# Two transformer layers with sliding-window attention on one core: chunks of 512 tokens, attention of a chunk between the matmuls of its left neighbour's MLP

## The chip, the cores and the metric

The kernel runs on one core of a Trainium2 chip. The metric is the device time of one execution in microseconds (us). A core has five engines with a queue of their own each, worked off in order: PE (matmul), ACT (activation functions), DVE (vector), POOL (GpSimd) and SP (here it only issues DMAs). Engines wait for each other through semaphores. Matmuls write into PSUM, eight banks of 512 fp32 columns; the other operands lie in SBUF.

## The reference

```python
def _A_ref(x, wqkv, wo):
    B, S, D = x.shape                       # 1, 2048, 576
    H = 32; Dh = D // H; W = 256
    qkv = (x @ wqkv).reshape(B, S, 3, H, Dh).transpose(2, 0, 3, 1, 4)
    q, k, v = qkv[0], qkv[1], qkv[2]
    scores = jnp.einsum("bhqd,bhkd->bhqk", q, k) * (Dh ** -0.5)
    mask = (idx[:, None] - idx[None, :] >= 0) & (idx[:, None] - idx[None, :] < W)
    p = _softmax(jnp.where(mask[None, None], scores, -1e9), axis=-1)
    o = jnp.einsum("bhqk,bhkd->bhqd", p, v)
    return o.transpose(0, 2, 1, 3).reshape(B, S, D) @ wo
def _B_ref(x, w1, b1, w2, b2):
    y = _layernorm(x, axis=-1)
    h = _gelu(jnp.einsum("bsd,df->bsf", y, w1) + b1)      # F = 4608, tanh form
    return jnp.einsum("bsf,fd->bsd", h, w2) + b2

for _ in range(2):
    x = x + _A_ref(_layernorm(x, axis=-1), A_wqkv, A_wo)
    x = x + _B_ref(_layernorm(x, axis=-1), B_w1, B_b1, B_w2, B_b2)
```

Inputs and weights are bf16. 32 heads of 18 channels; a query sees itself and the 255 keys before it. Both layers use the same weights.

## The kernel before

The tokens are 16 tiles of 128. The residual stream x_res stays in SBUF in fp32. Every operation is recorded by a small scheduler (class Sched): it notes which names a step reads and writes, derives the semaphore waits, and each engine then runs its steps in the order in which the code recorded them. So the order of recording is the order of execution on each engine.

There are four stages, one after the other: attention, MLP, attention, MLP, each over all tiles; at a seam the first tiles of the next stage are prepared in the last ones of the stage before (hooks A_HOOK_T and M_HOOK_TC).

Attention works by tile t, group g of four heads, and pair pr of two heads: 512 steps in all. A step scores (L538) multiplies the pair's keys of up to three key tiles with the queries, each head in its own 32 rows of the PE array; expo (L553, ACT) exponentiates 128 keys x up to 768 values; masks (L559 and L563, POOL) clear the triangles; pv (L580) multiplies with V, where a column of ones gives the sum of the softmax; norm (L601, L606, DVE) divides. Two score slots of two banks alternate. Between the steps come the projections of tiles to come: Q and K by tile pairs (L478, emptied by DVE at L488), V (L503, L512), the output projection (L628, L634). The layer norm is statistics (L391, L393), a square root on ACT (L410, L413), and normalisation (L421); five DMA transposes of 128x128 per tile on SP's queue (L431 for the normalised x, L615 for the attention's output) put the channels on the partitions.

The MLP goes by pairs of tiles (256 tokens) and pairs of 128 hidden channels: mm1 (L811) into one of three banks, then the gelu in six steps on ACT and DVE, the main lines of which are

```python
e.activation(g_xb, bank(b), ACT.Identity, bias=b1col, scale=1.0)      # L827, ACT
e.tensor_tensor(g_sq, g_xb, g_xb, ALU.mult)                           # L836, DVE
e.tensor_scalar(g_sq, g_sq, GELU_A, 1.0, op0=ALU.mult, op1=ALU.add)   # L842, DVE
e.tensor_tensor(g_u, g_sq, g_xb, ALU.mult)                            # L849, DVE
e.activation(g_sg, g_u, ACT.Sigmoid, scale=GELU_C)                    # L855, ACT
e.tensor_tensor(hT, g_xb, g_sg, ALU.mult)                             # L864, DVE
```

then mm2 (L914) into four banks per tile pair, into which a matmul with a row of ones has put b2 (L875); resid (L928) adds the result to x_res. w1 lies in SBUF as a whole; w2 is fetched anew for each pair of tiles, 144 KB at a time, by POOL (L893).

## Time and profile before

| | us |
|---|---|
| median of three runs | 1291.88 (1291.74 to 1292.63) |
| span of the profiled execution | 1289.2 |
| from the first instruction to PE's first matmul | 53.1 |
| attention 1, 53 to 347, and attention 2, 698 to 965 | 294 and 267 |
| MLP 1, 347 to 690, and MLP 2, 965 to 1275 | 343 and 310 |

The times of the runs are those of the device for an execution; the span is from the first to the last instruction of one execution under the profiler, whose own device time is not listed, so the runs' median stands beside the span. Stages are read from the first and last starts of their lines. Instructions are shown as engine, line, operation, output<-input, number; "busy" is the time in which the engine executed something; "idle before" is the time that the engine stood idle just ahead of a group, with who ended it. PEclk is the share of full speed that TensorE's clock was granted.

### The profile page before, as it was taken

How to read it: one execution, taken by the hardware profiler on the slowest of the kernel's cores; microseconds unless marked ns; L12 is line 12 of the kernel's file. 1: busy time of each engine (PE TensorE's matmuls, PEld its weight loads, DVE VectorE, ACT ScalarE, POOL GpSimd, SP SyncE). 2: the span in 40 equal slices, each digit the busy share in tenths (PEclk: the TensorE clock that was granted, in tenths of full speed). 3: DMA queues.
4: the chain of work that ended last, by engine and by line, in shares of the span. 5: the costliest groups of instructions: out<-in, count | busy, mean ns of one | idle time of the engine just before them, and what ended most of it. 6: DMA issues, size and time to landing. Idle time of an engine off the chain costs nothing.

```text
span 1289.2 us, 34293 instructions
## 1 busy us (share of the span) xinstructions
PE 1147.9 (89%) x12928; PEld 853.7 (66%) x12928; DVE 830.6 (64%) x2600; ACT 798.0 (62%) x1409; POOL 718.6 (56%) x1609
## 2 busy tenths in 40 slices
PE   0399999989699999999998999998959999999995
PEld 0256666655487777878884666665538888888884
DVE  3466666654377777778776666665527777777774
ACT  2057777777465655754664777777747666666663
POOL 8046777767454445543443777776745555555552
PEclk9999898887599999999998998998859999999998
DMA  9401101100154545553540110101005655556652
GB/s 278 136 18 23 22 21 22 21 19 16 48 150 136 143 131 139 153 147 109 143 136 15 22 23 20 22 21 22 17 17 157 159 156 153 151 159 158 158 148 75
DMA packets 116247, 118.02 MB, mean 92 GB/s; under 512 B 91249, under 2 KB 94450, under 8 KB 115506
## 3 DMA queue, kind: packets, MB, share of 16 engines
q0 software_dynamic: 37312, 97.38, 27.8%
q1 hardware_dynamic: 76800, 15.79, 6.0%
q10 hardware_dynamic: 1970, 2.66, 0.8%
q8 instruction: 103, 1.69, 0.6%
q14 instruction: 62, 0.51, 0.1%
HBM read 95.27 MB, written 2.36 MB: 76 GB/s over the span
## 4 chain that ended last, share of the span: by engine, by line
PE 74%; ACT 6%; DVE 5%; SPq 5%; DMA 4%; POOL 3%; issue 2%; ACTq 0%; POOLq 0%; DVEq 0%
PE ps L811 23%; PE ps L914 22%; PE ps L478 11%; PE ps L538 7%; PE ps L580 5%; ACT arena L553 5%; PE ps L628 4%; SPq L615 4%; DMA arena<-arena 2%; DVE st_all L391 2%; DVE x_res L928 2%; PE ps L503 2%; DMA x_res<-in_A_x_dram 1%; POOL arena L559 1%; SPq L431 1%
## 5 line engine op out<-in xcount | busy, mean ns | idle before, releaser
L553 ACT ACTIVATE arena<-ps 128x768 bf16<-128x768 f32 (+2 forms) x512 | 377.5, 773 | 180.4 <-PE ps L538 172.2
L893 POOL DMA_DIRECT2D w_sb<-in_B_w_dram x576 | 308.6, 541 | 295.9 <-PE ps L914 285.5
L827 ACT ACTIVATE arena<-ps,b1col 128x256 bf16<-128x256 f32 x576 | 241.3, 470 | 204.3 <-PE ps L811 196.1
L811 PE MATMUL ps<-xnT,w_sb 128*128 128x256 bf16 x2880 | 365.2, 275 | 0.0
L914 PE MATMUL ps<-w_sb,arena 128*128 128x288 bf16 x2304 | 331.1, 287 | 2.6 <-DVE arena L864 2.5
L559 POOL TENSOR_SCALAR_AFFINE_SELECT arena<-arena 128x256 bf16<-128x256 bf16 x512 | 212.6, 416 | 207.7 <-ACT arena L553 206.9
L811 PEld LDWEIGHTS ps<-xnT,w_sb 128*128 128x128 bf16 x2880 | 284.1, 99 | 42.5
L914 PEld LDWEIGHTS ps<-w_sb,arena 128*128 128x128 bf16 x2304 | 224.3, 98 | 57.9 <-DVE arena L864 4.5
L538 PE MATMUL ps<-arena 32*128 32x128 bf16 x2880 | 180.4, 231 | 23.6 <-ACT arena L553 12.3
L855 ACT ACTIVATE arena<-arena 128x512 bf16<-128x512 bf16 x288 | 181.0, 628 | 27.5 <-DVE arena L849 27.1
L488 DVE CAST arena<-ps 128x128 bf16<-128x128 f32 x512 | 124.6, 285 | 113.0 <-PE ps L478 105.8
L836 DVE TENSOR_TENSOR arena<-arena 128x512 bf16<-128x512 bf16 x288 | 121.6, 422 | 111.8 <-ACT arena L827 111.5
L563 POOL TENSOR_SCALAR_AFFINE_SELECT arena<-arena 128x256 bf16<-128x256 bf16 x448 | 181.9, 406 | 0.0
L538 PEld LDWEIGHTS ps<-arena 32*128 32x128 bf16 x2880 | 87.0, 96 | 121.3 <-issue 64.2
L580 PE MATMUL ps<-arena 128*128 128x32 bf16 x2880 | 158.5, 181 | 2.3 <-POOL arena L563 1.1
L478 PE MATMUL ps<-xnT,wq_pad 128*128 128x256 bf16 x640 | 102.7, 299 | 53.3 <-DMA xnT<-xn 53.1
L580 PEld LDWEIGHTS ps<-arena 128*128 128x128 bf16 x2880 | 107.2, 98 | 61.4 <-issue 7.6
L849 DVE TENSOR_TENSOR arena<-arena 128x512 bf16<-128x512 bf16 x288 | 122.5, 425 | 9.8
L864 DVE TENSOR_TENSOR arena<-arena 128x512 bf16<-128x512 bf16 x288 | 120.5, 418 | 2.8 <-ACT arena L855 2.8
L478 PEld LDWEIGHTS ps<-xnT,wq_pad 128*128 128x128 bf16 x640 | 58.3, 104 | 63.4 <-issue 53.4
L478 PE MATMUL ps<-xnT,wk_pad 128*128 128x256 bf16 x640 | 97.1, 287 | 0.2
L842 DVE TENSOR_SCALAR arena<-arena 128x512 bf16<-128x512 bf16 x288 | 84.9, 295 | 9.9
(52 smaller groups left out, 608.6 us busy)
## 6 DMA issues: line engine op xcount, KB each, us to landing
w_sb<-in_B_w_dram POOLq DMA_DIRECT2D x576, 144.0 KB, 2.5
xnT<-xn SPq DMA_TRANSPOSE x320, 2.9
w_sb<-in_B_w_dram POOLq DMA_DIRECT2D x4, 1152.0 KB, 8.8
x_res<-in_A_x_dram POOLq DMA_DIRECT2D x1, 4032.0 KB, 17.6
arena<-arena SPq DMA_TRANSPOSE x160, 2.4
out_dram<-x_res POOLq DMA_DIRECT2D x16, 144.0 KB, 2.8
arena<-in_A_wqkv_dram ACTq DMA_DIRECT2D x4, 288.0 KB, 3.9
wv_sb<-in_A_wqkv_dram ACTq DMA_DIRECT2D x4, 144.0 KB, 5.4
```

Of the source, the lines that this page charges most:

```text
L478: ins = e.matmul(bank(pb)[:, gi * 256:(gi + 1) * 256], wpad[:, c, g * 128:(g + 1) * 128], xnT[:, xs, c, 0:256], start=(c == 0), stop=(c == ...
L488: S.add("dve", lambda e, i=i, s_=s_: e.tensor_copy(dstT[:, s_, g0:g0 + NGR, :], src[:, :, i, :]), reads=[f"pb{pb}"], writes=[f"{which}{s_} ...
L538: ins = e.matmul(psS[:, slot, jj, b * 128:(b + 1) * 128], kT[32 * j:32 * j + 32, sk, g, :], qT[32 * j:32 * j + 32, sq, g, :], start=True, ...
L553: S.add("act", lambda e: e.activation(pT[:, sp_, :, b0 * 128:384], psS[:, slot, :, b0 * 128:384], ACT.Exp, scale=SCALE), reads=[f"pb{2 * s ...
L559: S.add("pool", lambda e: e.affine_select(pT[:, sp_, :, 256:384], pT[:, sp_, :, 256:384], pattern=[[0, 2], [1, 128]], compare_op=ALU.is_ge ...
L563: S.add("pool", lambda e: e.affine_select(pT[:, sp_, :, 0:128], pT[:, sp_, :, 0:128], pattern=[[0, 2], [-1, 128]], compare_op=ALU.is_gt, f ...
L580: ins = e.matmul(bank(ob)[:, jg * 32:(jg + 1) * 32], pT[:, sp_, jj, b * 128:(b + 1) * 128], vA[:, sv, h, :], start=(bi == 0), stop=(bi == ...
L811: ins = e.matmul(bank(b)[:, k * 256:(k + 1) * 256], w1_sb[:, c, fc * 128:(fc + 1) * 128], xnT[:, xs, c, 0:256], start=(c == 0), stop=(c == ...
L827: S.add("act", lambda e, k=k, fc=fc: e.activation(g_xb[:, r, k * 256:(k + 1) * 256], bank(b)[:, k * 256:(k + 1) * 256], ACT.Identity, bias ...
L855: S.add("act", lambda e: e.activation(g_sg[:, r, :], g_u[:, r, :], ACT.Sigmoid, scale=GELU_C), reads=[f"gw{r}"], writes=[f"gw{r}"])
L893: S.add(cfg.get("W2ENG", "pool"), lambda e, sl=sl, fc=fc: e.dma_start(w2_sb[:, sl, :], B_w2[fc * P:(fc + 1) * P, :]), writes=[f"w2s{sl}"], ...
L914: ins = e.matmul(bank(ybanks(i)[hh])[:, 0:DHALF], hT[:, hs, k * 256 + i * 128:k * 256 + (i + 1) * 128], w2_sb[:, sls[k], hh * DHALF:(hh + ...
```

## The change

The program is written anew. The unit is a chunk of 512 tokens (four tiles), four chunks a layer, eight in all (k = 0 to 7). Pass k computes the attention of chunk k and the MLP of chunk k-1; k = 8 has the MLP alone. Chunk 4 is the first of layer 2, which needs only what is behind it of layer 1. A pass consists of:

- ln1: rstd and normalisation of chunk k+1, and its transposes
- G_part for hidden half 0: 18 chunks of mm1 (five matmuls of 512 columns each) into banks 0 to 3, each emptied by one gelu with bias on ACT
- E_part 0, called E0 below: heads 0 to 15 of chunk k in 12 units, with mm2 of half 0 (24 pieces of six matmuls, one bank pair 5 and 6) and QK pieces of chunk k+1 (bank 7) shared out as fill
- G_part and E_part (E1) for hidden half 1 and heads 16 to 31; E1 has mm2 of three tiles
- the tail, T below: transposes of the attention's output, the last QK group, output projection and second norm tile by tile, the transposes for the MLP, then the rest of mm2 and the V pieces as fill

A unit is scores for four heads into banks 0 to 3, one bank a head, two exps of 128x1024, two or three masks on POOL, and, two units later, PV into bank 4. ACT's table is switched by hand between the gelu set and one that has exp and ln; rstd is now exp(-ln/2). w1 and w2 are both streamed by SP for each chunk: w1 in four slots of 512 hidden channels, w2 in halves. b2 is added to x_res by POOL. A transposing DMA covers 128x640. x is loaded in bf16 and copied to fp32 by POOL. The ring of semaphores and the names of reads and writes are as before; waits of PE on PE are left out.

```diff
-    def scores(t, g, pr, slot, ktl):
...
-                    for jj in range(2):
-                        j = 2 * pr + jj
-                        ins = e.matmul(psS[:, slot, jj, b * 128:(b + 1) * 128],
-                                       kT[32 * j:32 * j + 32, sk, g, :],
-                                       qT[32 * j:32 * j + 32, sq, g, :],
-                                       start=True, stop=True, tile_position=(32 * j, 0))
...
+    UNITS = [[(0, 0, 3, 0), (-2, 0, 1, 384)], [(1, 1, 3, 128), (3, 3, 1, 0)], [(-1, 0, 2, 0), (2, 2, 2, 256)]]
...
+    def scores(k, g, u):
...
+            for (so, qo, nq, col) in parts:
+                s = (k * CT + so) % KS
+                for j in range(4):
+                    ins = e.matmul(psS[:, j, col:col + nq * 128], kT[32 * j:32 * j + 32, g, s, :],
+                                   qT[32 * j:32 * j + 32, g, qo * 128:(qo + nq) * 128],
+                                   start=True, stop=True, tile_position=(32 * j, 0))
...
+        for h2 in range(2):
+            S.add("act", lambda e, h2=h2: e.activation(pT[:, sl, 2 * h2:2 * h2 + 2, lo:hi], psS[:, 2 * h2:2 * h2 + 2, lo:hi],
+                                                       ACT.Exp, scale=SCALE),
+                  reads=[f"pb{2 * h2}", f"pb{2 * h2 + 1}"], writes=[f"p{sl}h{h2}"])
...
+        S.add("sp", lambda e: e.dma_start_transpose(dst[:, :, i * 128:(i + 1) * 128], xn[:, sl, :]),
+              reads=[f"xn{sl}"], writes=[f"{dname}{i}"], dma="t", ring=8)
...
+        S.add("act", lambda e: e.activation(hT[:, fl, :], bank(bnk)[:, 0:CW], ACT.Gelu_apprx_tanh, bias=b1col[:, f:f + 1]),
+              reads=[f"pb{bnk}", "b1"], writes=[f"h{fl}"])
...
+    def E_part(k, hf, base, byg):
...
+        for n, (g, u) in enumerate(units):
+            sls.append(scores(k, g, u))
+            if n >= 2:
+                gg, uu = units[n - 2]
+                pv(k, gg, uu, sls[n - 2])
...
+            run_fill(q, (left + pend) / (len(units) - n))
...
+    for k in range(NK + 1):
...
+        if nxt:
+            ln1(k + 1)
+        if km >= 0:
+            G_part(km, 0, (0, 1, 2, 3))
+        base = mm2_fill(km, 0, range(CT)) if km >= 0 else []
+        byg = {g: qk_items(k + 1, g) for g in range(3)} if nxt else {}
+        E_part(k, 0, base, byg)
+        if km >= 0:
+            for pr in range(NFH // 2):
+                w2_load(1, pr)
+            G_part(km, 1, (0, 1, 2, 3))
...
+        E_part(k, 1, base, byg)
+        for i in range(CT):
+            att_T(i)
...
+        for i in range(CT):
+            outproj(k, i, ((0, 1), (2, 1))[i % 2])
+            ln_stats(ts[i])
+            ln_rstd(ts[i], True)
+            if i > 0:
+                ln_norm_T(ts[i - 1], xnTm, "xm")
+        ln_norm_T(ts[CT - 1], xnTm, "xm")
...
+        for it in fill:
+            it[1]()
```

Three places show how the order moves. First PE within attention. Before, in a tile of the first layer (L538 scores, L580 PV, L478 Q, L503 V):

```order
L478 MATMUL ps<-xnT,wq_pad 128x256 x5
L538 MATMUL ps<-arena 128x128 x6
L580 MATMUL ps<-arena 128x32 x6
L503 MATMUL ps<-wv_sb,xnT 128x288 x5
L538 MATMUL ps<-arena 128x128 x6
```

Now, in E0 of pass 1 (L388 scores, L426 PV, L491 mm2, L329 Q and K):

```order
L491 MATMUL ps<-w_sb,hT 128x288 x18
L388 MATMUL ps<-qT,kT 128x256 x8
L426 MATMUL ps<-vA,pT 128x20 x16
L491 MATMUL ps<-w_sb,hT 128x288 x12
L329 MATMUL ps<-xnTa,wq_pad 128x512 x5
L388 MATMUL ps<-qT,kT 128x384 x4
L388 MATMUL ps<-qT,kT 128x128 x4
L426 MATMUL ps<-vA,pT 128x20 x16
```

A score step has grown from six matmuls to eight wider ones, and matmuls of the MLP stand between the scores of two units.

Second PE at the end of pass 1, from the last PV of E1 to the rest of mm2 (L464 is the output projection, L356 V):

```order
L426 MATMUL ps<-vA,pT 128x20 x32
L329 MATMUL ps<-xnTa,wq_pad 128x512 x5
L329 MATMUL ps<-xnTa,wk_pad 128x512 x5
L491 MATMUL ps<-w_sb,hT 128x288 x6
L356 MATMUL ps<-wv_sb,xnTa 128x288 x5
L464 MATMUL ps<-wo_sb,attT 128x288 x40
L491 MATMUL ps<-w_sb,hT 128x288 x6
L356 MATMUL ps<-wv_sb,xnTa 128x288 x5
```

The output projections of all four tiles stand together, with two QK pieces, one mm2 piece and one V piece ahead of them, and the rest of the fill behind.

Third SP's queue. Before, from the end of the first attention over the MLP to the second attention (L431 normalised x, L615 the attention's output):

```order
L431 DMA_TRANSPOSE xnT<-xn 128x128 x5
L615 DMA_TRANSPOSE arena<-arena 128x128 x10
L431 DMA_TRANSPOSE xnT<-xn 128x128 x95
L615 DMA_TRANSPOSE arena<-arena 128x128 x5
L431 DMA_TRANSPOSE xnT<-xn 128x128 x5
```

Now, at the end of pass 1 (L309 and L311 w1, L316 w2, L446 the attention's output, L302 normalised x):

```order
L309 DMA w_sb<-in_B_w_dram 128x4x512
L311 DMA w_sb<-in_B_w_dram 64x512
L446 DMA_TRANSPOSE attT<-attq 128x5x128 x4
L302 DMA_TRANSPOSE xnTm<-xn 128x5x128 x4
L316 DMA w_sb<-in_B_w_dram 128x2x576 x9
L302 DMA_TRANSPOSE xnTa<-xn 128x5x128 x4
```

One transposing DMA stands for five, and the weights' loads, which were POOL's, stand between the transposes on the same queue.

1232 lines of the change are left out of this document (402 added, 830 removed).

## The prediction

> **What bounds it now.** The shares of the page come first, then a table by stage.
>
> ```profile
> span 1289.2 us, 34293 instructions
> PE 1147.9 (89%) x12928; PEld 853.7 (66%) x12928; DVE 830.6 (64%) x2600; ACT 798.0 (62%) x1409; POOL 718.6 (56%) x1609
> PE 74%; ACT 6%; DVE 5%; SPq 5%; DMA 4%; POOL 3%; issue 2%; ACTq 0%; POOLq 0%; DVEq 0%
> ```
>
> PE holds 89% of the span and 74% of the chain that ends last. Where it does not, the stages tell:
>
> ```profile
> core 0: us, PE busy (x) PEld busy (x) DVE busy (x) ACT busy (x) POOL busy (x), PEclk, DMA share, GB/s
> 38.00:53.00 15.00, 0.00 (x0) 0.00 (x0) 1.50 (x4) 0.98 (x1) 0.00 (x0) 1.00 0.40 107
> 128.00:300.00 172.00, 164.26 (x2495) 105.46 (x2492) 103.81 (x396) 126.99 (x162) 120.92 (x317) 0.91 0.10 21
> 300.00:347.00 47.00, 33.48 (x469) 20.45 (x468) 14.66 (x55) 26.33 (x36) 25.71 (x71) 0.58 0.07 15
> 965.00:1275.00 310.00, 305.30 (x2623) 255.14 (x2621) 230.43 (x610) 197.88 (x434) 161.94 (x302) 1.00 0.57 153
> ```
>
> Up to 53 us PE does nothing. Attention proper and the MLP keep PE busy 95% and 98%; the seam between them (300 to 347) has 71%, at clock 0.58. So the change can gain in three ways: less PE work, shorter seams, a shorter start.
>
> **What a PE operation costs.** A matmul's own duration is latency; the price is the distance of starts.
>
> ```profile
> 203.43 0.34 PE L538 MATMUL ps<-arena 32*128 32x128 bf16 x6
> 203.70 0.32 PE L580 MATMUL ps<-arena 128*128 128x32 bf16 x6
> 203.86 0.71 PE L478 MATMUL ps<-xnT,wq_pad 128*128 128x256 bf16 x5
> 204.50 0.28 PE L538 MATMUL ps<-arena 32*128 32x128 bf16 x4
> ...
> 452.06 1.25 PE L811 MATMUL ps<-xnT,w_sb 128*128 128x256 bf16 x10
> ...
> 453.15 1.14 PE L914 MATMUL ps<-w_sb,arena 128*128 128x288 bf16 x8
> ...
> 454.14 1.25 PE L811 MATMUL ps<-xnT,w_sb 128*128 128x256 bf16 x10
> ```
>
> Ten matmuls of 256 columns take 1.09 us (452.06 to 453.15), so 512 columns take 0.218; eight of 288 columns take 0.99, 0.124 each. PV takes 0.16 for six, 0.027 each, and its columns hardly matter: 20 in place of 32 is costed at the same. QK takes 0.64 for five where 5 x 0.109 is 0.55, so about 0.1 goes into the change to the row-tiled scores, and the same again on the way back. Six scores of 128 columns take 0.27; one behind the other they would take 6 x 0.055 = 0.33 and a switch. In pairs, as the two heads use different rows of the array, they take 0.16 and a switch of 0.1: pairs run together.
>
> **Less PE work.** The columns of mm1, mm2, QK, V and the output projection stay as they are (five matmuls of 512 for ten of 256). Scores go four heads at a time: a unit has 384+128 columns per head, 0.235 when the four run together, 0.87 if they don't. I take 0.235, since pairs do it now; with two switches 0.43. A full pass of the new loop costs PE: mm1 180 x 0.218 = 39.2; mm2 288 x 0.124 = 35.7; QK 80 x 0.218 = 17.4; V and output projection 80 x 0.124 = 9.9; scores 24 x 0.43 = 10.3; PV 384 x 0.027 = 10.4. Sum 122.9. What a pass costs beyond it are waits, and these need the other engines' prices:
>
> ```profile
> L553 ACT ACTIVATE arena<-ps 128x768 bf16<-128x768 f32 x448 | 347.6, 814 | 127.5 <-PE ps L538 125.2 <-POOL arena L563 0.8 <-POOL arena L559 0.5
> L553 ACT ACTIVATE arena<-ps 128x512 bf16<-128x512 f32 x32 | 18.5, 597 | 12.3 <-PE ps L538 12.3
> L827 ACT ACTIVATE arena<-ps,b1col 128x256 bf16<-128x256 f32 x576 | 241.3, 470 | 204.3 <-PE ps L811 196.1 <-DVE arena L864 8.1
> L559 POOL TENSOR_SCALAR_AFFINE_SELECT arena<-arena 128x256 bf16<-128x256 bf16 x512 | 212.6, 416 | 207.7 <-ACT arena L553 206.9
> L340 POOL TENSOR_SCALAR_AFFINE_SELECT mask_diag<-mask_diag 128x128 bf16<-128x128 bf16 x1 | 0.3, 287 | 0.1
> L488 DVE CAST arena<-ps 128x128 bf16<-128x128 f32 x512 | 124.6, 285 | 113.0 <-PE ps L478 105.8
> L512 DVE CAST arena<-ps 128x288 bf16<-128x288 f32 x64 | 29.0, 454 | 9.5 <-PE ps L503 8.9
> L928 DVE TENSOR_TENSOR x_res<-ps,x_res 128x576 f32<-128x576 f32 x32 | 23.1, 741 | 11.2 <-PE ps L914 11.1
> L391 DVE BATCH_NORM_STATS2 st_all<-x_res 128x6 f32<-128x288 f32 x128 | 58.1, 454 | 24.0 <-DMA x_res<-in_A_x_dram 20.1
> L421 DVE TENSOR_SCALAR xn<-x_res,mv_all,rs 128x576 bf16<-128x576 f32 x64 | 41.5, 670 | 0.1
> ```
>
> ACT takes 0.85 ns more per element (814-597 over 256), so an exp of 1024 takes 1.03; two in a row overlap by 0.1: 1.95 a unit. gelu, L827 stretched to 512, takes 0.69 (were it dearer, it stays hidden up to mm1's 1.09 per chunk). DVE empties 512 columns in 0.69. POOL masks 512 elements in 0.67 and 1024 in 1.2, so a unit's two masks (1.3 to 1.9) fit beside the exps.
>
> **E0 and E1, the two attention parts of a pass (12 units each).** The four score banks exist once, so the next unit's scores wait for both exps: 0.45 (scores to the end) + 0.1 + 1.95 = 2.5 us a unit at least; behind the waiting scores PE's queue holds that unit's PV and fill, and ACT waits for the scores. PE's own unit is scores 0.43, PV 0.43 and its fill. I walked the order unit by unit. E0: three mm2 pieces (2.22) give 3.08; the first two lack PV (2.65). On top: mm2 tile 3 waits 0.85 for its residual add (one bank pair), two QK pieces in a row wait 0.85 for bank 7 to be emptied, the one-piece unit 10 is lifted to 2.5, and the last PV waits for its own exps and masks (4.3 for the last unit). The first unit takes 3.4, its exp being behind the table load:
>
> ```profile
> 265.73 1.28 ACT L413 ACT_TABLE_LOAD   x1
> 267.03 0.30 ACT L413 ACTIVATE sd<-mv_all,eps_b 128x8 f32<-128x8 f32 x1
> 267.34 1.28 ACT L553 ACT_TABLE_LOAD   x1
> 268.64 1.51 ACT L553 ACTIVATE arena<-ps 128x768 bf16<-128x768 f32 x2
> ```
>
> A load costs 1.28, and the next activation stands 0.02 behind it. The Trainium skill, "ScalarE: Activation LUTs", § What ACT_TABLE_LOAD costs, counts 2.66 us with a drain; by that page the two loads ahead of exps would cost a pass 2.8 more, some 20 in all, and these rows show no such drain.
>
> E0 is then 3.4+2.65+3x3.08+3.4+3.9+2.7+3.1+3.9+2.5+4.3 = 39.1, and 1.0 ahead of it for the last gelu: 40.1. E1, with 18 mm2 and 8 QK pieces: 1.0+3.4+2.65+3x3.08+2.7+3.1+2x2.7+2x2.5+4.3 = 36.8. The two mm1 parts are 2 x 90 x 0.218 and 0.4 for the start: 39.6.
>
> **T, the tail** (transposes, output projection, second norm), is a chain that crosses five engines:
>
> ```profile
> L431 SPq DMA_TRANSPOSE xnT<-xn x320: 1094/1230/2576, 38.1 to 1216.9; - x160
> xnT<-xn SPq DMA_TRANSPOSE x320, 2.9
> q1 hardware_dynamic: 76800, 15.79, 6.0%
> q0 software_dynamic: 37312, 97.38, 27.8%
> ```
>
> A transposing DMA of one 128x128 block takes SP 1.23 and lands after 2.9. The new ones carry five blocks. The bounds: 1.23 if the price is per DMA, 6.15 if it is per block. The queue's data took 6.0% of 1289 us for 480 blocks, 0.16 each; I take 1.23 + 4 x 0.16 = 1.9, landing 1.7 later. Then: normalise 0.75; first transpose landed at 4.35; first projection 5.6; DVE has per tile 0.74 + 1.12 + 0.67, and the last rstd comes from ACT at 15.2, the last transpose lands at 19.5. The V pieces, which share bank 7, are emptied by ACT, and ACT's queue has them behind all four rstd pairs; PE's queue has the remaining mm2 pieces behind those V pieces. They run from 15.7 to about 23. So T is 23 for 16.5 of PE work; the transposes stay covered.
>
> **The clock.** The half-speed share was 0.09 in attention; over T and the last three units of each E (38 us) that is 3.4 a pass; bounds are 0 (the MLP's row at 1.00) and 10 (T at the seam's 0.58). The Trainium skill, "TensorE: Matmul & The Clock Gate", Part 1, lets the gate fall only after an idle window of about 3.4 us; the 0.91 at 95% busy PE does not bear that out.
>
> **Start and end.**
>
> ```profile
> x_res<-in_A_x_dram POOLq DMA_DIRECT2D x1, 576.0 KB, 7.2
> ...
> 1272.26 2.13 PE L914 MATMUL ps<-w_sb,arena 128*128 128x288 bf16 x16 [0.55 <-DVE arena L864]
> ```
>
> The first chunk lands at about 7, four statistics take 4.5, norms and four transposes end near 22; V and QK of chunk 0 (8 x 0.62 + 16 x 1.09 = 22.4, V from the first tile on, DVE's other statistics in the way for some 4) end at 46. Chunk 0 has no MLP to fill with: its units are bound by exps (2.1, 2.5, 1.7), 58 with the ends, and T 23. Now 14.8 us lie behind the end of the last matmul (1274.4); I keep 14.
>
> **The sum.** Start 46; pass 0: 81; five full passes of 40.1+36.8+39.6+23+3.4 = 142.9: 714.5; pass 4, whose chunk has no left keys, 24 x 0.055 + 96 x 0.027 = 3.9 less: 139.0; pass 7 without QK and V, its units at the exps' 2.5: 2 x 34 + 39.6 + 20 + 2 = 129.6; the MLP alone 2 x (19.6+1+17.8) + 14 = 91. Together 1201.1. The median of the runs stands 2.7 above the profiled span of before (1291.9 against 1289.2), which I add: **1204**.
>
> **What hides the rest.** Weights: a pass reads 10.6 MB. q0 moved 97.38 MB in 27.8% of the span, 272 GB/s when busy; a 655 KB block of w1 needs 2.4 us and PE uses it up in 4.36. The dropped DVE gelu steps, the bias matmuls (64 x 0.124 = 8 us of PE, in the sum by their absence) and POOL's DMA issues were beside PE. The b2 additions on POOL lie beside mm1. On SP's queue the tail's transposes stand behind w1 loads that mm1 released before E1, and the next chunk's transposes behind nine w2 loads (2.65 MB, 10 us at that rate), 30 us before their first use.
>
> **Rivals.**
> Transposes priced by the block (slower): in T, SP issues eight of them, T becomes 2.45 + 8 x price once that exceeds 23. From (23 + 88/8 - 2.45)/8 = 3.9 us each the change loses; at 6.15 T is 51.7, in eight passes +230 and +17 at the start: 1450. For it: one block costs 1.23 now. Against: only 0.16 of that is data. Chance 0.07.
> Row groups do not run four at a time, so that the change isn't what it says: 192 units x 0.64 = +122, 1325. Against: pairs run together now. 0.05.
> Weights too slow: rows of 1 KB in w1 at half the rate take 4.8 where PE takes 4.36; nine blocks a pass give +32, with w2 beside them up to +60: 1235 to 1263. 0.08.
> The waits overlap: my walk adds each stall in full; if half of the 20 us a pass go, 8 x 10 less, 1124; if all of them, 1044. 0.18.
> The clock stays up: 8 x 3.4 less, 1177. By the page's rule on the gate this is the case, and the 0.91 row speaks against it. 0.08.
> Waits that I overlooked eat all of it: about 1290, 0.02.
> My forecast, 1150 to 1255: 0.52.
>
> Within 0.2% (2.6 us) a measurement can't tell the kernel from no change. Faster by more, the forecast and the three rivals under 1289: 0.86; same: 0.02; slower: 0.12. The range, 1110 to 1320, takes in all but the two slower rivals and a third of the overlapping waits (0.18).
>
> **What will show it.** PE's first matmul near 18 to 22; 24 units of exps at 2.5 to 3.1 from scores to scores; the four score matmuls of a quad starting within some ns; a five-block transpose near 1.9 on SP; from the last PV of a pass to its next mm1 23; mm1 parts at 19.6 without gaps. Wrong it is if SP's transposes take over 4, if mm1 waits for w1, or if clock rows fall under 0.9 in the E parts.

## The result, and the profile after

| | us |
|---|---|
| before, median of four runs | 1292.26 (1291.74 to 1292.73) |
| after, median of four runs | 1175.72 (1174.12 to 1179.94) |
| ratio after to before, 95% interval | 0.9102 (0.9086 to 0.9119) |
| forecast | 1204, range 1110 to 1320 |
| span of the profiled execution after | 1178.2 (that run: 1179.94) |

The changed kernel takes 9% less, 28 us less than forecast. The shares of its page:

```profile
span 1178.2 us, 22128 instructions
PE 1028.5 (87%) x9312; PEld 580.0 (49%) x9312; DVE 306.8 (26%) x615; ACT 654.1 (56%) x927; POOL 353.2 (30%) x429
PEclk9897899999999899999999999999999989998899
PE 73%; DVE 10%; ACT 8%; issue 5%; POOL 3%; DMA 1%; SPq 0%; POOLq 0%; DVEq 0%
```

PE's busy time fell by 119 us (1147.9 to 1028.5), the span by 111: PE stands idle about as long as before, 150 us against 141, and what went is time in which it worked, or ran at half speed (the mean clock rose from 0.934 to 0.961). DVE's busy time fell by 524 us and POOL's by 365, but their shares of the chain that ends last did not fall (DVE 5% before and 10% now, POOL 3% and 3%), so that drop is not itself the gain. One pass, as windows of the trace (columns as in the table by stage above): mm1 of half 0, E0, mm1 of half 1, E1, T, and in the last row the MLP alone that ends the program.

```profile
272.30:292.67 20.37, 19.59 (x93) 8.73 (x91) 2.20 (x5) 14.90 (x29) 0.00 (x0) 1.00 0.88 234
292.67:331.84 39.17, 35.13 (x462) 22.43 (x463) 9.32 (x16) 25.79 (x26) 18.41 (x24) 1.00 0.24 72
331.84:353.89 22.05, 21.27 (x96) 9.11 (x93) 0.71 (x2) 12.40 (x19) 0.00 (x0) 0.92 0.38 108
353.89:389.73 35.84, 32.63 (x435) 19.96 (x436) 12.89 (x26) 24.51 (x25) 18.41 (x24) 1.00 0.06 18
389.73:414.69 24.96, 20.32 (x134) 12.78 (x131) 12.22 (x26) 5.58 (x17) 5.60 (x4) 0.86 0.49 116
1097.72:1178.20 80.48, 77.21 (x468) 46.31 (x468) 6.06 (x8) 28.58 (x39) 0.00 (x0) 0.96 0.35 112
```

The attention parts now have PE busy 90% and 91% beside 25 us of exps on ACT. What is left lies in T and at the end of each attention part. The rows of PE, then ACT, then SP at the end of E1 of pass 1 and in the T that follows it (start, duration, engine, line, number, and in brackets the wait ahead of it):

```profile
248.71 0.55 PE L426 MATMUL ps<-vA,pT 128*128 128x20 bf16 x16 [1.46 <-POOL pT L407]
...
260.80 0.78 PE L356 MATMUL ps<-wv_sb,xnTa 128*128 128x288 bf16 x5
261.42 0.90 PE L491 MATMUL ps<-w_sb,hT 128*128 128x288 bf16 x6
265.06 0.79 PE L356 MATMUL ps<-wv_sb,xnTa 128*128 128x288 bf16 x5 [2.74 <-ACT vA L365]
...
271.68 0.79 PE L356 MATMUL ps<-wv_sb,xnTa 128*128 128x288 bf16 x5 [0.50 <-ACT vA L365]
272.30 1.89 PE L479 MATMUL ps<-xnTm,w_sb 128*128 128x512 bf16 x8
```

```profile
262.28 0.20 ACT L288 ACTIVATE rstd<-lnv 128x1 f32<-128x1 f32 x1
264.27 0.20 ACT L286 ACTIVATE lnv<-mv_all 128x1 f32<-128x1 f32 x1 [1.78 <-DVE mv_all L282]
264.50 0.20 ACT L288 ACTIVATE rstd<-lnv 128x1 f32<-128x1 f32 x1
264.61 0.39 ACT L365 ACTIVATE vA<-ps 128x288 bf16<-128x288 f32 x1
```

```profile
250.07 5.19 SPq L446 DMA_TRANSPOSE attT<-attq  x4
260.28 7.77 SPq L302 DMA_TRANSPOSE xnTm<-xn  x4
```

ACT waits 1.78 us for the fourth tile's statistics, and the V piece that PE had put into bank 7 from 260.80 on is emptied only behind that rstd, at 264.61. PE waits 2.74 us, then works off the other pieces one by one until mm1 starts at 272.30. SP had issued the last transpose by 268.05. A five-block transpose costs SP 1.30 (5.19 for four).

### The profile page after: what moved, and what is told of

Its sections match the earlier page's. It is cut to its first block, busy times and chain, and to the rows that moved or that the text cites. A ratio compares the mean times of both kernels' runs of the same rounds, so it can differ in the third digit from the quotient of the medians.

```text
span 1178.2 us, 22128 instructions
## 1 busy us (share of the span) xinstructions
PE 1028.5 (87%) x9312; PEld 580.0 (49%) x9312; DVE 306.8 (26%) x615; ACT 654.1 (56%) x927; POOL 353.2 (30%) x429
## 4 chain that ended last, share of the span: by engine, by line
PE 73%; DVE 10%; ACT 8%; issue 5%; POOL 3%; DMA 1%; SPq 0%; POOLq 0%; DVEq 0%
PE ps L479 27%; PE ps L491 21%; PE ps L329 10%; ACT pT L396 5%; PE ps L426 5%; PE ps L388 5%; PE ps L356 4%; DVE st_all L280 3%; DVE x_res L454 3%; POOL pT L407 2%; DVE xn L299 2%; PE ps L464 1%; ACT hT L483 1%; ACT vA L365 1%; DVE mv_all L282 1%
## 5 line engine op out<-in xcount | busy, mean ns | idle before, releaser
L407 POOL TENSOR_SCALAR_AFFINE_SELECT pT<-pT 128x512 bf16<-128x512 bf16 (+1 forms) x368 | 277.4, 776 | 633.2 <-ACT pT L396 622.2
L396 ACT ACTIVATE pT<-ps 128x1024 bf16<-128x1024 f32 (+2 forms) x384 | 351.7, 967 | 168.7 <-PE ps L388 168.5
L479 PE MATMUL ps<-xnTm,w_sb 128*128 128x512 bf16 x1440 | 323.6, 387 | 6.0 <-DMA xnTm<-xn 6.0
L491 PE MATMUL ps<-w_sb,hT 128*128 128x288 bf16 x2304 | 317.5, 290 | 8.7 <-DVE x_res L454 8.1
L483 ACT ACTIVATE hT<-ps,b1col 128x512 bf16<-128x512 f32 x288 | 195.6, 687 | 138.9 <-PE ps L479 138.8
L491 PEld LDWEIGHTS ps<-w_sb,hT 128*128 128x128 bf16 x2304 | 218.6, 99 | 76.7 <-DVE x_res L454 11.3
L479 PEld LDWEIGHTS ps<-xnTm,w_sb 128*128 128x128 bf16 x1440 | 142.8, 100 | 180.8 <-issue 19.8
L426 PE MATMUL ps<-vA,pT 128*128 128x20 bf16 x2880 | 102.8, 172 | 21.1 <-POOL pT L407 20.6
L426 PEld LDWEIGHTS ps<-vA,pT 128*128 128x128 bf16 x2880 | 85.7, 96 | 59.2 <-issue 41.6
L388 PE MATMUL ps<-qT,kT 32*128 32x384 bf16 (+2 forms) x1408 | 74.6, 279 | 37.2 <-ACT pT L396 25.5
L356 PE MATMUL ps<-wv_sb,xnTa 128*128 128x288 bf16 x320 | 58.6, 325 | 49.5 <-ACT vA L365 29.2
L329 PE MATMUL ps<-xnTa,wk_pad 128*128 128x512 bf16 x320 | 86.9, 406 | 16.3 <-DVE kT L335 6.3
L329 PE MATMUL ps<-xnTa,wq_pad 128*128 128x512 bf16 x320 | 84.7, 398 | 5.6 <-DVE kT L335 5.0
L388 PEld LDWEIGHTS ps<-qT,kT 32*128 32x128 bf16 x1408 | 22.3, 92 | 101.6 <-ACT pT L396 61.5
L356 PEld LDWEIGHTS ps<-wv_sb,xnTa 128*128 128x128 bf16 x320 | 31.5, 108 | 71.3 <-ACT vA L365 37.6
L329 PEld LDWEIGHTS ps<-xnTa,wk_pad 128*128 128x128 bf16 x320 | 28.6, 102 | 54.5 <-ACT qT L337 9.4
```

What stands on the lines that cost most here:

```text
L329: ins = e.matmul(bank(bnk)[:, 0:CW], wpad[:, c, g * 128:(g + 1) * 128], xnTa[:, c, :], start=(c == 0), stop=(c == KD - 1))
L356: ins = e.matmul(bank(bnk)[:, 0:DHALF], xnTa[:, c, i * 128:(i + 1) * 128], wv_sb[:, c, hh * DHALF:(hh + 1) * DHALF], start=(c == 0), stop= ...
L388: ins = e.matmul(psS[:, j, col:col + nq * 128], kT[32 * j:32 * j + 32, g, s, :], qT[32 * j:32 * j + 32, g, qo * 128:(qo + nq) * 128], star ...
L396: S.add("act", lambda e, h2=h2: e.activation(pT[:, sl, 2 * h2:2 * h2 + 2, lo:hi], psS[:, 2 * h2:2 * h2 + 2, lo:hi], ACT.Exp, scale=SCALE), ...
L407: S.add("pool", lambda e, ap=ap, pat=pat, sgn=sgn, kind=kind: e.affine_select(ap, ap, pattern=pat, compare_op=(ALU.is_ge if kind == "d" el ...
L426: ins = e.matmul(bank(B_O)[:, o:o + VW], pT[:, sl, j, col + qi * 128:col + (qi + 1) * 128], vA[:, sv, 4 * g + j, :], start=(first and n == ...
```

## The experiments

The theory after the result: the change gains because the fill lies beside the exps; what it leaves lying is V behind rstd, the last unit of each attention part, and the start. The rivals were those of the prediction. Each run up to "The start" changes one place of the changed kernel, the last three join several edits; all are compared with its median of 1175.72. Its runs scatter by 6 us, so differences under 4 us are not read. What the one-pass gelu, the shorter seams and the streamed weights are worth one by one was not tried.

**The interleaving alone.** All fill goes behind the last PV of its part.

```diff
-            run_fill(q, (left + pend) / (len(units) - n))
-        for c, f in q:
-            f()
         for n in (len(units) - 2, len(units) - 1):
             gg, uu = units[n]
             pv(k, gg, uu, sls[n])
+        for c, f in q:
+            f()
```

> The changed kernel without the interleaving alone: all mm2 and QK pieces of an attention part run behind its last PV, no instruction is added or dropped. Theory (the units are bound by the exps, 2.5 us each with four score banks, and the fill lies beside them for nothing): a part takes 3.4 + 10 x 2.5 + 4.3 = 32.7 us and then its fill, 24.4 (first) or 22.1 (second) us of PE and up to 5 us of waits for the one bank pair and bank 7, so 57 to 62 and 55 to 60 us instead of 39.2 and 35.8: +37 to +48 in each of six passes, about +30 in pass 7, +16 in pass 0, 1444 to 1510, slower than the kernel before. Rival (the gain of the change comes from shorter seams, fewer PE columns and the one-pass gelu, and the interleaving hides little): +100 at most, 1275 or less, still no slower than before.

Measured: 1600.44 us, 1.2381 of the kernel before (1.2356 to 1.2405). The page's clock row, and windows over E0's units, its fill, and behind the next mm1 E1's units and the fill with T:

```profile
PEclk9655859599595986959979697886978769786899
```

```profile
394.95:429.25 34.30, 13.51 (x289) 7.71 (x290) 2.15 (x6) 25.79 (x26) 18.42 (x24) 0.55 0.01 3
429.25:460.78 31.53, 26.57 (x175) 17.14 (x174) 7.20 (x11) 0.00 (x0) 0.00 (x0) 0.95 0.25 76
481.14:515.44 34.30, 13.42 (x287) 7.53 (x288) 2.14 (x6) 24.52 (x25) 18.42 (x24) 0.54 0.06 18
515.44:573.02 57.58, 45.49 (x279) 27.43 (x281) 23.12 (x46) 5.60 (x18) 5.60 (x4) 0.89 0.24 59
```

The 12 units alone take 34.3 us against 39.2 and 35.8 with the fill among them: 5 and 1.5 us were the price of work that takes 31.5 and, with 24 off the last row for T, 33.6 by itself. The units alone ran mostly at half speed; at full speed they might be shorter, and that price higher. So the theory's mechanism holds, and without it the rest of the change (fewer PE columns, the one-pass gelu, no seams) loses to the kernel before. The size expected was too small, by at least 90 us: E0 with its fill took 65.8 where 62 was the most expected, E1 67.9 instead of at most 60, and pass 0 took 125.0 instead of 81.4 where 16 more were expected. In all three the clock has a part that was left out: PE, busy for 13.5 of 34.3 us, was granted half speed in most of those units (0.55) and in part of what followed (0.95 and 0.89), and in pass 0 for 102.4 us on end.

**Row groups.** First the heads one after the other, in the order of issue only:

```diff
-            for (so, qo, nq, col) in parts:
-                s = (k * CT + so) % KS
-                for j in range(4):
+            for j in range(4):
+                for (so, qo, nq, col) in parts:
+                    s = (k * CT + so) % KS
```

> The changed kernel with the scores of a unit issued head by head (both column groups of one head, then the next head) instead of four heads at a time; same matmuls, same banks. Theory (four heads in four row groups run together, 512 columns for the price of 0.235 us; two matmuls in a row on the same row group don't): scores of a unit take 0.87 to 1.07 instead of 0.43, and as exps wait for them in every unit, 192 x 0.45 to 0.64 = +86 to +122: 1262 to 1298. Rival (the four don't run together anyway): no change, 1172 to 1180. Middle case (the last matmul of a head runs beside the first of the next one): +0.25 to 0.4 a unit, 1223 to 1252.

Measured: 1177.56 us (0.9116 of before, 0.9084 to 0.9148), no change. That would be the rival's result, but the trace shows something else: the eight matmuls of a unit still take 0.41 us. Their starts, in the order of time, are the four of 384 columns at 212.623, .631, .637 and .644, then the four of 128 columns at 212.797 to .816, though in the queue each one of 128 columns stands ahead of the next head's 384. So this kernel did not run its heads in series, and the run says nothing on the price. A second one takes the row groups away: every head uses rows 0 to 31, with the data of the group's first head.

```diff
-                    ins = e.matmul(psS[:, j, col:col + nq * 128], kT[32 * j:32 * j + 32, g, s, :],
-                                   qT[32 * j:32 * j + 32, g, qo * 128:(qo + nq) * 128],
-                                   start=True, stop=True, tile_position=(32 * j, 0))
+                    ins = e.matmul(psS[:, j, col:col + nq * 128], kT[0:32, g, s, :],
+                                   qT[0:32, g, qo * 128:(qo + nq) * 128],
+                                   start=True, stop=True, tile_position=(0, 0))
```

> The changed kernel with all four heads of a unit scored on the rows of the first head (rows 0 to 31, keys and queries of head 0 of the group four times): the scores of the other three heads are left out, the matmuls keep their number and shape. The run with heads issued one after the other took no longer, and its trace shows the matmuls of the four row groups starting 7 ns apart although another matmul stood between them. Theory (each row group works through its own matmuls beside the others, so that the price is per row group): with one row group left, a unit's 2048 columns take 0.87 to 1.07 us instead of 0.43, in 192 units +84 to +123 us, 1260 to 1298. Rival (row groups are not what runs together; a matmul of 32 rows simply starts every few ns): no change, 1172 to 1180.

Measured: 1297.50 us (1.0039 of before, 1.0023 to 1.0056), +121.8. PE's timeline for the eight scores of one unit: the changed kernel, heads in series, one row group.

```profile
213.25 0.40 PE L388 MATMUL ps<-qT,kT 32*128 32x384 bf16 x8 [0.78 <-ACT hT L483]
```

```profile
212.62 0.41 PE L388 MATMUL ps<-qT,kT 32*128 32x384 bf16 x8
```

```profile
244.87 1.04 PE L388 MATMUL ps<-qT,kT 32*128 32x384 bf16 x8 [0.78 <-ACT hT L483]
```

0.64 us more in each of 192 units is 122.9, close to the whole difference. Pass by pass it is not so even, and that the sums meet is in part luck: 24 units x 0.64 would be 15.4, and passes 1 to 7 are 9.7 to 16.8 longer, but pass 0 is 25.5 longer, with PE at half speed for 61.4 us on end. Without the four row groups the change gains nothing. The theory stands; the order within a unit made no difference here.

**Transposes by the block.** Each five-block DMA becomes five of one block (the same for the attention's output).

```diff
-        S.add("sp", lambda e: e.dma_start_transpose(dst[:, :, i * 128:(i + 1) * 128], xn[:, sl, :]),
+        for c in range(KD):
+            S.add("sp", lambda e, c=c: e.dma_start_transpose(dst[:, c, i * 128:(i + 1) * 128], xn[:, sl, c * 128:(c + 1) * 128]),
```

> The changed kernel with each five-block transposing DMA issued as five of one 128x128 block. It tests the formula that the prediction had for transposes that are priced by the block: tail = 2.45 + 8 x price. Theory (each DMA costs SP 1.23, as in the kernel before): 6.15 a tile, tail 51.7 instead of 23.4, +28 in seven passes and +34 in pass 7, and 10 to 15 more at the start: 1410 to 1430. Rival (SP's price is that of the wait for data, and single blocks in a row cost 0.2 to 0.6 each): up to 3 a tile, tail at most 26.5: 1172 to 1205.

Measured: 1562.81 us (1.2094 of before, 1.2068 to 1.2120). SP's timeline from a last PV at 323.7 on, each row a run of DMA issues:

```profile
324.72 25.33 SPq L448 DMA_TRANSPOSE attT<-attq  x20
350.15 26.16 SPq L303 DMA_TRANSPOSE xnTm<-xn  x20
376.40 5.01 SPq L317 DMA_DIRECT2D w_sb<-in_B_w_dram  x9
381.50 26.36 SPq L303 DMA_TRANSPOSE xnTa<-xn  x20
407.96 0.53 SPq L310 DMA_DIRECT2D w_sb<-in_B_w_dram  x1
```

A block costs 1.27 to 1.32, mm1 starts at 378.0, so T is 54.3 where the formula gave 51.7. The formula held, and still the kernel is over 130 us above what was expected. Most of that stands in the last two rows: w1's next block is issued at 407.96, behind the next chunk's 20 transposes, and mm1 waits for it. The first mm1 part takes 32.7 us in pass 1 and 37 to 38 in passes 2 to 6 instead of 19.2, some 105 us in all. Queued behind transposes was not only the tail but the weights.

**V in the tail: the bank.** V pieces alternate between banks 7 and 4.

```diff
-        return [(0.6, lambda i=i, hh=hh: v_piece(k, i, hh, ev=ev)) for i in range(CT) for hh in range(2)]
+        return [(0.6, lambda i=i, hh=hh: v_piece(k, i, hh, bnk=(B_X, B_O)[hh], ev=ev)) for i in range(CT) for hh in range(2)]
```

> The changed kernel, with the V pieces of the tail going alternately to banks 7 and 4 (bank 4 is free once the last PV of the pass has been divided); nothing moves in any queue. Theory (the prediction's step: ACT empties V only behind the fourth rstd pair, at about 16 us into the tail, and the pieces then go one by one through one bank): the wait for the fourth rstd stays, but behind it a piece no longer waits 0.5 to 0.9 us for its bank, seven pieces at 0.62 with the mm2 pieces between them, so the tail falls from 23.2 to about 20 in seven passes, -20 to -25 us, near 1152. Rival 1 (the tail is bound by norms and transposes, not by V): no change, 1172 to 1180. Rival 2 (it is the order behind rstd alone that costs, not the bank): -0 to -8.

**V in the tail: the order.** Fill goes between the tiles, ahead of their rstd.

```diff
             ln_stats(ts[i])
+            for _ in range((0, 2, 2, 2)[i]):
+                if nxt and fill:
+                    fill.pop(0)[1]()
             ln_rstd(ts[i], True)
```

> The changed kernel, with the tail recorded in another order: of the fill (mm2 and V pieces), two items each go behind the statistics of the second, third and fourth tile, ahead of that tile's rstd, so that ACT empties three to four more V pieces before the last rstd; the V pieces still have the one bank. Theory: by the time of the fourth rstd six of the twelve items are done, the other six need about 5 us from there, so mm1 starts near 19.5 to 20.5 instead of 23.2 after the last PV: -20 to -25 us, near 1152. Rival (the output projections, now behind V pieces in PE's queue, come 1.4 to 2 us later per tile and DVE's chain of residual, statistics and norm with them): -0 to -7, or up to +10. Second rival (norms and transposes bind the tail anyway): no change.

Measured: 1151.11 (0.8906, 0.8867 to 0.8944) and 1149.52 (0.8887, 0.8859 to 0.8915), 25 and 26 us less. From the last PV to mm1 passes 1 to 6 take 20.3 to 21.9 and 19.4 to 20.8 instead of 23.2 to 25.0. PE's last rows before mm1, with two banks and with the other order:

```profile
258.70 1.39 PE L356 MATMUL ps<-wv_sb,xnTa 128*128 128x288 bf16 x10
260.14 15.05 PE L479 MATMUL ps<-xnTm,w_sb 128*128 128x512 bf16 x68
```

```profile
266.87 0.79 PE L356 MATMUL ps<-wv_sb,xnTa 128*128 128x288 bf16 x5 [0.50 <-ACT vA L365]
268.66 6.64 PE L479 MATMUL ps<-xnTm,w_sb 128*128 128x512 bf16 x30 [1.00 <-DMA xnTm<-xn]
```

With two banks mm1 follows V without a wait; in the other order it waits 1.00 for its transposes, so there the norms' chain has become the limit. The two edits shorten the same stretch in different ways: with two banks PE still waits 2.13 us for the emptying behind the last rstd, but one more V piece has gone ahead of it and the waits of 0.50 between pieces are gone; in the other order the wait of 2.74 is gone and one of 0.50 is left. The rivals that had T bound by norms or transposes from the start fall.

**POOL beside DVE.** The additions of b2 wait for the last transpose (`reads=[f"x{t}", "b2", "xm3"]`).

> The changed kernel, with POOL's four additions of b2 in each tail made to wait for the last transposing DMA instead of for each tile's own norm, so that none of them runs beside DVE's statistics and norms of the tail. It measures what a POOL tensor operation costs DVE beside it. Theory (DVE is slowed while POOL works on the same memory: the last two norms took 2.33 us together where one alone takes 0.54): these two norms take 1.1 together and the last transpose lands 1.2 earlier; but V's wait behind rstd and the single bank bind the tail, so the time changes by less than 3 us (1172 to 1179). Rival (the last norm binds the tail): -1.2 in seven or eight passes, about -9. Second rival (the norms are slow for another reason): the two norms still take 2.3.

Measured: 1175.30 us (0.9094, 0.9069 to 0.9119), no change, as the theory had it. The last two norms of a tail take 1.23 together instead of 2.33; it is the last one alone, which ran beside an addition, that falls from 1.68 to 0.58. DVE's 60 norms from x_res, changed kernel and this one (busy, mean ns, idle before):

```profile
L299 DVE TENSOR_SCALAR xn<-x_res,mv_all,rstd 128x576 bf16<-128x576 f32 x60 | 40.7, 707 | 14.3 <-ACT lnv L286 8.2 <-ACT rstd L288 5.2
```

```profile
L299 DVE TENSOR_SCALAR xn<-x_res,mv_all,rstd 128x576 bf16<-128x576 f32 x60 | 32.8, 576 | 15.4 <-ACT lnv L286 9.3 <-ACT rstd L288 5.2
```

**The last unit of an attention part.** One piece is held back for the wait of 1.46 us ahead of the last PV.

```diff
-            run_fill(q, (left + pend) / (len(units) - n))
-        for c, f in q:
-            f()
+            run_fill(q, (left + pend - KEEP) / (len(units) - n))
         for n in (len(units) - 2, len(units) - 1):
+            if n == len(units) - 1:
+                for c, f in q:
+                    f()
```

> The changed kernel, with one fill piece (a QK piece of 1.09 us) of each attention part held back until after the second last PV, and the share of the other units made smaller by as much. In the trace PE waits 1.46 us there for the masks of the last unit. Theory (all of that wait can be filled): about 1.1 in each of 15 parts, -16 us. Rival (the units that lose the piece are already at the 2.5 us which the exps set, so PE's time saved there is only waited for earlier): 0 to -6 us. The last PV's wait falls from 1.46 to 0.4 in the theory; in the rival the scores of the last units wait longer for the exps.

Measured: 1161.27 us (0.8984, 0.8959 to 0.9009), 14 less, near the theory's 16. E0 takes 37.3 instead of 39.2, E1 34.8 instead of 35.8; T became 0.7 to 1.0 longer in passes 1 to 5, since in E1 the held piece's evacuation now stands on DVE ahead of the last division.

**The start.** DVE clears wq_pad and wk_pad while it waits for x; statistics of tiles 4 to 15 come behind the k evacuations.

```diff
-    S.add("pool", lambda e: e.memset(wq_pad[:, :, :], 0.0), writes=["wqm"])
+    S.add("dve", lambda e: e.memset(wq_pad[:, :, :], 0.0), writes=["wqm"])
...
-    for t in range(CT, NT):
-        ln_stats(t, x_in, f"xin{t}")
...
         qk_piece(0, g, "k", bnk=(4, 6)[g % 2], ev="dve")
+    for t in range(CT, NT):
+        ln_stats(t, x_in, f"xin{t}")
```

> The changed kernel with another start: wq_pad and wk_pad are cleared by DVE while it waits for x, POOL clears of xn only the pad columns, and DVE's statistics of tiles 4 to 15 stand behind the k evacuations of chunk 0. In the trace DVE's four first norms took 2.39 us each while POOL cleared these tensors, and PE waited 3.81 us for a k evacuation that stood behind 24 statistics. Theory: norms at 0.5 to 0.8 each, PE's first matmul 3 to 4 earlier and no wait for k: first scores near 42 to 44 instead of 51: 1166 to 1169. Rival (the four norms are slow for another reason, or DVE's clearing is as slow beside POOL): only the wait for k goes, first scores at 46 to 48, 1171 to 1173. Second rival (the statistics now stand ahead of something that pass 0 needs): no gain.

Measured: 1182.58 us (0.9147, 0.9128 to 0.9167), 7 more. Scores did start at 44.0 instead of 51.1, but pass 0 took 91.2 instead of 81.4: the norms of chunk 1 stood on DVE behind eleven us of statistics, and PE waited for their transposes (its timeline):

```profile
63.51 1.91 PE L329 MATMUL ps<-xnTa,wq_pad 128*128 128x512 bf16 x4 [7.74 <-DMA xnTa<-xn]
```

The second rival held. The norms of chunk 0 did fall, from 9.3 to 4.2 for the four. What POOL did beside them in the changed kernel was mostly the clearing of vA (11.58 to 17.18), not of wq_pad and wk_pad, which it had cleared by 11.64.

The tails of passes 1 to 6 also became longer, 25.3 on average instead of 24.0, and this goes with the clock, whose record says when PE ran at half speed: 44 us of it fell into these six tails, and 27 in the changed kernel. In the five kernels that have the same order of PE's work in the tail (the changed kernel, this one, the late additions, heads in series, one row group), T of passes 1 to 6 takes

| half speed within T | T, us | tails |
|---|---|---|
| none | 22.3 | 1 |
| one stretch of 3.41 us | 23.2 to 24.0 | 17 |
| two | 25.0 to 25.2 | 8 |
| three | 26.3 and 26.4 | 2 |
| four | 27.8 and 28.0 | 2 |

so each stretch costs T about 1.4. Why more of them fell into the tails of this run is open. By the same count, with one stretch in T, two banks save about 2.0 us a tail and the other order about 2.9; the rest of their gain is half speed that no longer fell into T and mm1.

**Together, without the start.** Both V edits, the late additions, the held piece, and the k evacuation of group 6 on ACT.

```diff
+            byg[6][1] = (1.08, lambda k=k: qk_piece(k + 1, 6, "k", ev="act"))
```

> Both edits of the V pieces (two banks, and two fill items ahead of the rstd of the second, third and fourth tile), the late additions of b2, and the piece held back in each attention part; the k evacuation of group 6, which then stood ahead of the last division on DVE and made the tail 0.5 to 0.9 longer, goes to ACT. Theory (with V out of the way the tail is bound by the chain of transposes, projections, residuals, statistics and norms, 18 to 18.5 us as in pass 7, and the late additions now count 1.2 of it): tail 19 to 20 instead of 23.4, -25 to -30; attention parts 1.9 and 1.0 shorter, -14 to -20 with the cleared DVE: 1125 to 1136. Rival (the edits share one gain: each removes waits after which PE's half-speed windows come, and the two V edits remove the same wait): no better than 1138 to 1145.

Measured: 1121.37 us (0.8669, 0.8647 to 0.8692), better than the range: T 19.1 to 19.3, E0 37.3, E1 34.8, and the mm1 parts of passes 2 to 6 all at 19.2. Its clock row shows why the sum is more than its parts:

```profile
PEclk9878799999999999999999999999999999998899
```

The clock record of the changed kernel's trace has 93.6 us at half speed in all, and eleven stretches of 3.41 us between 134 and 1011 us, one to three a pass; here there is none in that time. Each edit alone takes away its own: with the other order of V, and so without the wait of 2.74, the seven stretches left in passes 1 to 6 all begin within 1.7 us behind the last PV of an attention part, ahead of which the wait of 1.46 stands; with the piece held back, and so without that of 1.46, those left all lie in T, 15 to 17 us behind the last PV.

**With a new start.** In addition wq_pad and wk_pad are cleared by DVE as in the first try, x of chunk 0 is loaded ahead of the rest, wo last, and the statistics of tiles 8 to 15 stand behind E0 of pass 0; then the same with these statistics spread over its units.

```diff
+            if k == 0 and hf == 0 and 3 <= n < 11:
+                ln_stats(2 * CT + n - 3)
...
-        if k == 0:
-            for t in range(2 * CT, NT):
-                ln_stats(t)
```

> As the kernel before in this list, with the start rearranged: x of chunk 0 alone is loaded first, the other three chunks and wo behind the first four transposes; wq_pad and wk_pad cleared by DVE ahead of the statistics, the other small clears after the k scatter; statistics of tiles 4 to 7 ahead of the k evacuations and those of tiles 8 to 15 after the first attention part. Theory (the first transposes waited for the 5 MB loaded ahead of them, and in the first try at the start pass 0 lost what the start gained, because norms of chunk 1 stood behind twelve statistics): first scores at 37 to 42 instead of 49 to 51, pass 0 still 81 or less: 8 to 13 us under the run before it, 1113 to 1127. Rival (DVE's chain sets the start whatever is loaded): scores at 44 as in the first try, 5 to 7 us under it.

> The kernel of the run before with one thing moved: the statistics of tiles 8 to 15 stand one tile behind each of units 3 to 10 of pass 0's first attention part, not all eight behind that part. In the trace before, first scores came 10.3 us earlier (40.7 instead of 50.9), but PE then waited 6.1 us for a q evacuation that stood behind these 7.4 us of statistics on DVE, and pass 0 took 86.3 instead of 79.0. Theory (this queueing is all that was lost): pass 0 back at 79 to 80, first scores still at 40.7: 6 to 7 us less, 1112 to 1116. Rival (pass 0 is held up by PE at half speed after the start, whatever DVE does): 0 to -2, 1118 to 1122.

Measured: 1120.74 (0.8658, 0.8637 to 0.8679), no better than without, and 1111.43 (0.8611, 0.8591 to 0.8631). In the first, scores started at 40.7, and PE paid it back behind E0 (its timeline in pass 0):

```profile
77.47 2.31 PE L323 MATMUL ps<-xnTa,wk_pad 128*128 128x512 bf16 x5 [6.10 <-DVE qT L329]
```

In the second they start at 39.8, pass 0 takes 76.9, a little better than the 79 to 80 of its theory: the queue had cost the first try what its start had gained. This version beats the kernel before by 14% and the changed one by 64 us.

## Why the prediction was right, and where its terms were off

The sum was made for the span: 1201.1 against 1178.2. By its own terms:

| term | forecast | measured |
|---|---|---|
| start to first scores | 46 | 51.1 |
| pass 0 | 81 | 81.4 |
| five full passes | 714.5 | 704.6 |
| pass 4 | 139.0 | 133.8 |
| pass 7 | 129.6 | 126.9 |
| MLP alone | 91 | 80.5 |
| median minus span | 2.7 | -2.5 |

- **The walk through the units** held: E0 39.1 forecast, 39.2 measured; E1 35.8 and 35.8; mm1 19.6 a part against 19.2, or 20.9 where half speed fell in it; 1.0 ahead of the scores against 1.16. The stalls I added one by one are there (2.74 in T and 1.46 ahead of the last PV above; 0.79 for bank 7 and 0.85 for the residual add), so the rival that half of them overlap, 1124, is out.
- **Exp, gelu, masks**: the pair of exps takes 1.94 (1.95 forecast), a gelu 0.69. The first unit, forecast at 3.4, took 3.56 in the E1 of pass 1 and 3.25 in the E0 of pass 2. In that E1 the exps stand right behind the load:

```profile
213.22 1.28 ACT L510 ACT_TABLE_LOAD   x1
214.51 1.94 ACT L396 ACTIVATE pT<-ps 128x1024 bf16<-128x1024 f32 x2
217.26 1.94 ACT L396 ACTIVATE pT<-ps 128x1024 bf16<-128x1024 f32 x2 [0.81 <-PE ps L388]
```

  The exp starts 0.01 behind the end of the load; nothing stands between them, as in the row of before.
- **T** was 23 forecast and is 23.2 to 25.0 in passes 1 to 6, for the reason given, which both V edits confirm; without half speed it would be 22.3 by the table above. The price of a transpose, 1.9, was too high (1.30); it is covered, so the error cost nothing.
- **Four row groups** run together, at 0.40 a unit with the switch, and their price without that, +122, came out at +121.8, though not evenly over the passes (above).
- **The full passes and the clock.** Forecast were parts of 139.5 and 3.4 a pass for the clock; the measured mean is 140.9. Ten stretches of 3.41 us at half speed fall into these five passes, three in mm1, where each adds 1.7 (20.9 for 19.2), and seven in T, where each adds about 1.4: together 3.0 a pass, so the clock was priced about right. Its place was not: none fell into the units of E, and three fell into mm1. What was too dear by 1.6 a pass are the parts: mm1 takes 38.4 for its two halves instead of 39.6, and T at full speed 22.3 instead of 23. The 0.09 that the prediction calls the half-speed share is the share of clock lost; the time at half speed is twice that. The rival "the clock stays up" gave 1177 and so nearly the right time, but for the wrong reason: the clock did not stay up, and the end of the program and the offset made up the difference.
- **The end** is the largest error. Up to the start of the last matmul (1174.65) the MLP alone took 76.9 where the sum has 76.8. The 14 us behind it were taken over from before without asking what they were: there POOL's DRAIN instruction at the program's end stands from 1279.91 to 1288.99, 9.1 us of the 14.8, and here it takes 0.2. What makes it long was not tried; the kernel before issues its weights' and output's DMAs from POOL, this one from SP. Here SP sends each tile out as it is done, and the span ends 3.6 behind the last matmul's start. The last rows of the timeline:

```profile
1174.97 0.76 DVE L454 TENSOR_TENSOR xn<-ps,x_res 128x576 bf16<-128x576 f32 x1 [3.65 <-PE ps L491]
1175.76 0.33 SPq L502 DMA_DIRECT2D out_dram<-xn  x1
```

- **Pass 4** lost more than PE's 3.9: without left keys the exps are shorter too, and the units near the exps' 2.5 us follow (E0 36.4, E1 33.1).
- **The start** was short by 5: PE's first matmul came at 17.5, just ahead of the 18 to 22 forecast, but DVE's work was dearer than costed. DVE's groups by form, changed kernel and the kernel with the new start:

```profile
L299 DVE TENSOR_SCALAR xn<-hT,mv_all,rstd 128x576 bf16<-128x576 bf16 x4 | 9.3, 2386 | 0.0
L272 DVE COPY wk_pad<-w_sb 128x576 bf16<-128x576 bf16 x4 | 3.9, 1026 | 0.0
```

```profile
L293 DVE TENSOR_SCALAR xn<-hT,mv_all,rstd 128x576 bf16<-128x576 bf16 x4 | 2.7, 731 | 0.0
L266 DVE COPY wk_pad<-w_sb 128x576 bf16<-128x576 bf16 x4 | 1.0, 300 | 0.0
```

  I had taken norms at 0.67 from the row of before, without POOL's work beside them. In the changed kernel POOL clears vA beside the norms and works on DMA issues and casts of x beside the copies; with the new start it casts x beside the norms and stands idle beside the copies. With k evacuations behind all statistics PE then waited 3.8 us and ran QK at half speed up to 42.1.
- **The offset** added the before kernel's median minus its span. The profiled run of after is the slowest of its four (1179.94 for a span of 1178.2), so a median less than its span is a matter of which run was profiled, not of the kernel. Where both are listed for one run, its time stands 1.7 to 2.1 above its own span.
- **One figure was off without effect.** A block of w1 is 576 rows of 512, 590 KB and not 655, so it needs 2.2 us at the rate used and not 2.4; mm1 did not wait for w1.

## What to carry to other kernels

Work laid between the steps of a chain that another engine bounds was worth here what it costs alone, and more, because a PE that waited was also clocked down; so fill the last gaps too, where several small edits together gave more than their sum. In each such gap look at what stands ahead in the queue of the engine that empties the bank: recording a few V pieces ahead of ACT's rstd was worth as much as a second bank, and twice a step brought forward (the start) was lost again to twelve or eight statistics queued in front of what PE needed next. A term that is copied from the old kernel, such as its end, must be worked out anew when the code behind it is new.

## What the runs showed of the hardware

- Scores on different row groups do not keep the order of issue: matmuls of 384 columns of the next heads started 0.17 us ahead of a 128-column one issued before them, and a unit took 0.40 and 0.41 us in the two orders, 1.04 on one row group.
- Half speed comes in stretches of 3.41 us or a multiple, after partial waits of PE, not only after idle ones: a wait of 1.46 us was followed by one at the end of many attention parts (one began at 250.3, after the wait that ended at 248.71), and with the waits filled those of passes 2 to 6 were gone. The stretches lie on a grid of 3.41 us. Counted over that grid in passes 1 to 6 of the changed kernel and its twelve variants, a window at full speed was followed by half speed in all 64 cases in which rows of matmuls cover less than 0.42 of it, in 46 of 118 cases between 0.42 and 0.58, and in none of 2835 above; a window at half speed was followed by full speed only from 0.787 on. The kernel before does not fit this count: there windows covered to 0.89 and 0.93 were followed by half speed. So it is no rule of PE's rows alone, and what the clock goes by stays open.
- POOL work stretched some DVE operations and not others. Beside POOL's clears a bf16 norm took 2386 ns on average, and one of them 5.6 us: it stood from 11.72 to 17.34 beside a clear that ended at 17.18. Beside POOL's casts of x it took 731, a k copy 0.76 to 0.79 us, and with POOL idle the copy took 0.30. An fp32 norm that began just behind one of the additions of b2 took 1.68 us, and 0.54 to 0.58 without. Two statistics took 0.77 to 0.82 beside POOL's work and without it. The Trainium skill, "SBUF — State Buffer", § SBUF: two separate sides, has DVE and GpSimd share a port pair that one of them locks for a whole instruction, on DVE's side only in certain modes or with two inputs from SBUF. These durations agree with such a lock; the modes no trace here shows.
